# A recurrent segment loop: last K half in two banks, second scores moved, batched Q/K groups in column tiles

## The chip, the core and the metric

The kernel runs on one core of a Trainium2 chip. TensorE (PE) multiplies matrices into PSUM, which has eight banks of 512 float32 columns; VectorE (DVE) and ScalarE (ACT) read PSUM and write SBUF; GpSimd (POOL) works from SBUF to SBUF; SyncE (SP) issues the DMAs. Each engine works through its own list of instructions in order and waits on semaphores for the others. The metric is the device time of one execution in microseconds (us).

## The reference

Two layers follow one another on x of shape 1 x 2048 x 512, in bfloat16:

- Mixer A: `h = x + A(layernorm(x))`. A cuts the 2048 rows into 64 segments of 32 rows. To each segment 8 memory rows are put in front, so 40 rows. From them Q, K and V are computed for 32 heads of 128 (512 x 4096 weights each), causal softmax attention among the 40 rows (all rows see the 8 memory rows), and the output projection Wo (4096 x 512). The first 8 of the 40 output rows are the memory rows of the next segment, the other 32 are the result. So segment s + 1 can't start before the first output rows of segment s are there.
- Mixer B: `h + B(layernorm(h))`, a gated MLP: a 512 x 1792 projection with GELU, a layer norm of one half, a mixing over all 2048 rows with a 2048 x 2048 matrix, a gate, and an 896 x 512 projection.

## The kernel before, in words

After a start phase, in which weights are loaded and the first Q, K and V are made, the loop `for s in range(NSEG)` (line 945) runs over the 64 segments; a last phase does mixer B. The order of the instructions is written out by hand: the Python code records each operation with its engine, and what a recorded operation reads and writes (tokens such as a PSUM bank, or half of a tile) gives the semaphore waits. Two engines that read the same PSUM bank are also ordered one after the other. Nothing is rescheduled.

The work of a segment is split by rows of x. The recurrence needs the memory rows (8) and the first 24 rows of the segment, so these 32 rows are the stationary operand `hT` of four 32-column tiles of the PE, side by side, while 512 columns of the weights stream through each. Four such matmuls (one per tile) that run side by side are called a quad below. The last 8 rows of each segment ("ext" rows) depend on no memory and are computed in batches ahead of time: for 16 segments at once, 128 ext rows `hTe` are one operand. Their Q and K are made by "batched groups", one per segment of the loop (`qkx_group`, line 891, and `qkx_mm`, line 406: 16 matmuls of 128 x 128 over the whole array), and land in `QTx`; their V by `vx_group` and `vx_atoms`. Late segments (s from 48) have mixer B work in that place (`z2_group`).

The order of one segment on the PE:

- `QK` (line 501): Q and K of head halves b = 0 and b = 1, four quads each, in four banks. With `held` a quad uses the weights that the quad before it has loaded. Line 495 is a matmul with its weight load, line 496 one without. Among them `mem_out(s - 1, 1)` brings the second half of the memory rows.
- After each bank, `QK_evac` (512): ACT copies it to `Tst` (line 519), interleaving pairs of heads, and DVE transposes 32 x 32 blocks to `QT` or `KT` (line 532). The bank of the last K is copied and transposed in two halves, both once the bank is complete. DVE puts the mask into the scores' banks (line 544).
- `S_half(s, 0)` (546), the scores of half 0; ACT does the exponential (`sm_exp`, line 568). Four quads of V for half 0 and one for half 1; `V_evac(0)` on DVE (line 615); `sm_sums(0)`, the softmax sums by a matmul with ones (line 575 and 496); `S_half(s, 1)`; three quads of V for half 1; `sm_sums(1)`.
- ACT does a logarithm (`sm_ln`, 586) and an exponential (`sm_rcp`, 590) to get the reciprocal; the order on ACT is exp 0, ln 0, exp 1, rcp 0, ln 1, rcp 1. POOL copies the next segment's ext Q (`qx_copy`, 539) and normalises half 0 in two products (lines 594 and 598: the second for the ext columns). DVE evacuates V of half 1 and normalises half 1, in the same two products.
- The batched group in bank 3 (`XB`), then `PV_half` (lines 623 and 629) for both halves, in tiles of 32 rows. ACT and DVE bring the result out (`cT_evac`, 642 and 644), and DVE copies the batched group's bank to `QTx` (line 425).
- `WoX_mm` (707), a quad of ext V in most segments (433), `Wo` (line 495 with `f_cT`: quads of 256 columns), `part_evac` (671 on ACT, 673 on DVE), and `mem_out(s, 0)` (680, 685), the memory rows of the next segment.

Of the kernel before, what the change touches and what calls it, by code (L numbers as in the profile page):

```python
# [169 lines left out]
def fast_path(nc, st, keep, A_x, A_mem0, A_Wq, A_Wk, A_Wv, A_Wo, A_seg_len, B_w_in, B_w_sp, B_b_sp, B_w_out, out):  # L170
# [33 lines left out]
    def region(off, n):  # L204
        return arena[:, off:off + n]
# [5 lines left out]
    QTx = [region(4 * WSZ + i * QX, QX).rearrange("p (m s h k) -> p m s h k", m=2, s=CK, h=H) for i in range(2)]  # L211
# [269 lines left out]
    QKB = {(0, 0): 0, (0, 1): 1, (1, 0): 6, (1, 1): 7}  # L481
    SBK = (0, 1)
# [29 lines left out]
    def QK_evac(s, b, mi, parts=1):  # L512
        bank = QKB[(b, mi)]
        tb = mi
        n = 8 // parts
        for k in range(parts):
            tok = [("T", tb, 0), ("T", tb, 1)] if parts == 1 else [("T", tb, k)]
            cs = slice(64 * n * k, 64 * n * (k + 1))
            act(lambda e, cs=cs: e.activation(out=Tst[:, tb, cs].rearrange("p (hp i r) -> p hp i r", i=32, r=2),  # L519
                                              in_=ps[:, bank, cs].rearrange("p (hp r i) -> p hp i r", r=2, i=32), func=ACT.Copy),  # L520
                reads=[PB(bank)], writes=tok)
        for k in range(parts):
            tok = [("T", tb, 0), ("T", tb, 1)] if parts == 1 else [("T", tb, k)]
            src = Tst[:, tb, 64 * n * k:64 * n * (k + 1)].bitcast(U32)
            hs = slice(n * k, n * (k + 1))
            if mi == 0:
                dst = QT[:, b, hs, :, :].rearrange("p hp q r -> p (hp q r)").bitcast(U32).rearrange("p (hp q) -> p hp q", hp=n)[:, :, 8:40]
                wr = [("QT", b)]
            else:
                dst = KT[:, b, hs, :, :].rearrange("p hp q r -> p (hp q r)").bitcast(U32)  # L530
                wr = [("KT", b, 0), ("KT", b, 1)] if parts == 1 else [("KT", b, k)]
            dve(lambda e, dst=dst, src=src: e.transpose(out=dst, in_=src), reads=tok, writes=wr)  # L532
# [13 lines left out]
    def S_half(s, b):  # L546
        bank = SBK[b]
        j = s % CK
        buf = (s // CK) % 2
        rd = [("QT", b), ("KT", b, 0), ("KT", b, 1), ("QTe", b)]  # L550
        for g in range(4):
            for c in range(4):
                hp, r = 2 * c + g // 2, g % 2
                pe(lambda e, hp=hp, r=r, c=c, g=g: e.matmul(  # L554
                    ps[32 * c:32 * c + 32, bank, g * 40:(g + 1) * 40], lhsT=KT[:, b, hp, :, r], rhs=QT[:, b, hp, :, r],
                    start=False, stop=(g == 3), skip_group_check=True, tile_position=(0, 32 * c)),
                    reads=rd, writes=[PB(bank)])
        for c in range(4):
            h0 = 16 * b + 4 * c
            pe(lambda e, c=c, h0=h0: e.matmul(  # L560
                ps[32 * c:32 * c + 32, bank, 160:224], lhsT=QTx[buf][:, 1, j, h0:h0 + 4, :].rearrange("p h k -> p (h k)"),
                rhs=QT[:, b, 2 * c:2 * c + 2, 0:16, :].rearrange("p hp q r -> p hp r q"),
                start=False, stop=True, skip_group_check=True, tile_position=(0, 32 * c)),
                reads=rd + [("QTx", buf, 1, i) for i in range(8)], writes=[PB(bank)])
# [28 lines left out]
    def sm_norm(b, on):  # L593
        on(lambda e: e.tensor_tensor(out=E_sb[:, b, 0:160], in0=R_sb[:, b, :], in1=E_sb[:, b, 0:160], op=ALU.mult),
           reads=[("R", b), ("E", b)], writes=[("E", b)])
        ev = E_sb[:, b, 160:224].rearrange("p (g q) -> p g q", q=16)
        rv = R_sb[:, b, :].rearrange("p (g q) -> p g q", q=40)[:, :, 0:16]
        on(lambda e: e.tensor_tensor(out=ev, in0=rv, in1=ev, op=ALU.mult), reads=[("R", b), ("Ex", b)], writes=[("Ex", b)])

    def V_half(s, b, dcs=range(DC), held=None):  # L600
        bank = VB[b]
        sl = slot(s)
        for dc in dcs:
            for c in range(4):
                c0 = (16 * b + 4 * c) * DH
                pe(lambda e, dc=dc, c=c, c0=c0: tile_mm(e, ps[32 * c:32 * c + 32, bank, :], hT[:, sl, dc, :], w_v[:, dc, c0:c0 + 512],
                                                        dc == 0, dc == DC - 1, c, dc == held),
                   reads=[("hTx", (s // 4) % 3), ("hTm", s, dc // 2), ("W", 2, 2 * b), ("W", 2, 2 * b + 1)], writes=[PB(bank)])

    def V_evac(b, eng):  # L610
        bank = VB[b]
        if eng == "act":
            act(lambda e: e.activation(out=V_sb[:, b, :], in_=ps[:, bank, :], func=ACT.Copy), reads=[PB(bank)], writes=[("V", b)])
        else:
            dve(lambda e: e.tensor_copy(out=V_sb[:, b, :], in_=ps[:, bank, :]), reads=[PB(bank)], writes=[("V", b)])  # L615

    def PV_half(s, b):
        xb = s % NVX
        for g in range(4):
            for c in range(4):  # L620
# [5 lines left out]
                    reads=[("V", b), ("E", b)], writes=[PB(PVB[c])])  # L626
# [270 lines left out]

    def vx_group(ck, n):
# [12 lines left out]
    for ck, i0 in ((1, 10), (2, 0), (3, 0)):  # L911
# [3 lines left out]
        for i in range(i0, 16):  # L915
            qkx_group(ck, i)
# [28 lines left out]
    for s in range(NSEG):  # L945
# [15 lines left out]
        QK(s, 0, 0, (0, 1), 0, 3)  # L961
        if s > 0:
            mem_out(s - 1, 1)
        QK(s, 0, 1, (1, 0), 1, 2, None if s else 1)
        QK(s, 0, 0, (2, 3), 0, 3)
        QK_evac(s, 0, 0)
        mask_put(0)
        QK(s, 0, 1, (3, 2), 1, 2, 3)
        QK_evac(s, 0, 1)
        mask_put(1)  # L970
        for mi in range(2):
            QK(s, 1, mi, ((2, 0, 1, 3), (3, 0, 1, 2))[mi], (2, 3)[mi], (3, 2)[mi], (2, 3)[mi])
            lastop["qk"[mi]] = em.by_eng["pe"][-1]
            QK_evac(s, 1, mi, 1 + mi)
# [6 lines left out]
        V_half(s, 0, (0,))  # L981
        if s > 0:
# [25 lines left out]
        V_evac(1, "dve")  # L1008
        sm_norm(1, dve)
        if s == 0:  # L1010
# [1097 lines left out]
```

## Time and profile before

| | |
|---|---|
| median of 3 runs | 854.24 us (854.01 to 854.5) |
| the profiled execution | 853.86 us, its span 851.7 us |
| PE busy | 837.0 us, 98% of the span |
| DVE, ACT, POOL busy | 538.8, 427.1 and 159.8 us |
| chain that ended last | PE 95% |
| granted PE clock | 1.0 in every slice |

The span is the time from the first to the last instruction. The chain that ended last is followed back from the last instruction, at each step to what released it. A matmul's row gives the time of its start and a modelled length; matmuls overlap, so the distance from one start to the next is what a stage costs, and a PE that is always busy can still hold waits between starts.

### The profile page before, as it was taken

To read this page: it belongs to the slowest core of one execution; us is meant where nothing else is said; L and a number is where in the kernel's file an instruction comes from. 1 tells how busy PE (TensorE), PEld (TensorE's weight loads), DVE (VectorE), ACT (ScalarE), POOL (GpSimd) and SP (SyncE) were. 2 spreads that over 40 slices of the span, in tenths; PEclk is the share of its full clock that TensorE was granted. 3 is DMA by queue.
4 is the path that set the end of the run, shared out by engine and by line. 5 is a ranking of instruction groups with operands and counts; after the bars stand their busy time and mean duration, and the time that the engine had idled before them with its cause. 6 is when DMAs were issued, how large, how long until landed. Compare 5 with 4: busy or idle time off the path is not lost.

```text
span 851.7 us, 43893 instructions
## 1 busy us (share of the span) xinstructions
PE 837.0 (98%) x20921; PEld 447.0 (52%) x19133; DVE 538.8 (63%) x1256; ACT 427.1 (50%) x1151; POOL 159.8 (19%) x404
## 2 busy tenths in 40 slices
PE   6999999999999999999999999999999999999997
PEld 5754445555555555556555555555554544444443
DVE  3456677676666666676766666767666676553443
ACT  2455565656555655555655555565656566500000
POOL 5111121122121112121212121211112123200000
PEclk9999999999999999999999999999999999999999
DMA  9972322223212122121323222233322369032001
GB/s 319 379 227 59 75 56 57 54 47 82 57 34 75 34 65 62 26 72 47 64 58 85 55 74 51 81 70 85 91 57 80 96 184 366 2 112 105 33 12 40
DMA packets 105614, 77.21 MB, mean 91 GB/s; under 512 B 63304, under 2 KB 90960, under 8 KB 105424
## 3 DMA queue, kind: packets, MB, share of 16 engines
q1 hardware_dynamic: 105424, 74.35, 30.3%
q8 instruction: 159, 2.61, 1.3%
q14 instruction: 31, 0.25, 0.1%
HBM read 42.38 MB, written 21.59 MB: 75 GB/s over the span
## 4 chain that ended last, share of the span: by engine, by line
PE 95%; DMA 2%; SPq 1%; issue 0%; ACT 0%; DVE 0%; POOL 0%; POOLq 0%
PE f_ps L495 46%; PE f_ps L1183 11%; PE f_ps L496 8%; PE f_ps L414 6%; PE f_ps L707 4%; PE f_ps L1300 3%; PE f_ps L623 3%; PE f_ps L1176 2%; PE f_ps L433 2%; PE f_ps L775 2%; PE f_ps L554 1%; PE f_ps L575 1%; DMA f_arena<-in_A_Wk_dram 1%; PE f_ps L629 1%; PE f_ps L439 1%; PE f_ps L680 1%
## 5 line engine op out<-in xcount | busy, mean ns | idle before, releaser
L495 PE MATMUL f_ps<-f_arena,f_hT 128*32 128x512 bf16 x5120 | 359.5, 380 | 0.3
L495 PEld LDWEIGHTS f_ps<-f_arena,f_hT 128*32 128x32 bf16 x5120 | 117.0, 95 | 153.7 <-issue 63.0
L519 ACT ACTIVATE f_Tst<-f_ps 128x512 bf16<-128x512 f32 (+1 forms) x320 | 150.0, 510 | 77.5 <-PE f_ps L495 77.4
L495 PE MATMUL f_ps<-f_arena,f_cT 128*32 128x256 bf16 x3844 | 127.9, 272 | 0.7 <-ACT f_cT L642 0.5
L495 PEld LDWEIGHTS f_ps<-f_arena,f_cT 128*32 128x32 bf16 x3844 | 94.8, 96 | 27.3 <-ACT f_cT L642 18.2
L615 DVE CAST f_V_sb<-f_ps 128x512 bf16<-128x512 f32 x128 | 88.6, 692 | 25.4 <-PE f_ps L495 25.4
L1183 PE MATMUL f_ps<-f_arena 128*128 128x512 bf16 x448 | 100.9, 379 | 0.6 <-DMA f_arena<-wT_d 0.6
L532 DVE STREAM_TRANSPOSE f_QT<-f_Tst 128x256 uint32<-128x256 uint32 x128 | 57.0, 446 | 68.6 <-ACT f_Tst L519 68.5
L496 PE MATMUL f_ps<-f_arena,f_hT 128*32 128x512 bf16 x1024 | 99.8, 379 | 0.0
L539 POOL COPY f_QT<-f_arena 128x256 bf16<-128x256 bf16 x64 | 30.8, 482 | 313.3 <-PE f_ps L560 313.2
L642 ACT ACTIVATE f_cT<-f_ps 128x320 bf16<-128x320 f32 x128 | 49.0, 435 | 49.1 <-PE f_ps L629 49.1
L644 DVE TENSOR_SCALAR f_cT<-f_ps 128x320 bf16<-128x320 f32 x128 | 56.9, 487 | 25.4 <-PE f_ps L629 25.4
L532 DVE STREAM_TRANSPOSE f_KT<-f_Tst 128x128 uint32<-128x128 uint32 (+1 forms) x192 | 64.5, 349 | 12.9 <-ACT f_Tst L519 12.9
L1183 PEld LDWEIGHTS f_ps<-f_arena 128*128 128x128 bf16 x448 | 43.7, 98 | 53.4 <-DVE f_mv L723 1.0
L673 DVE CAST f_part<-f_ps 128x256 bf16<-128x256 f32 x64 | 27.2, 425 | 67.9 <-PE f_ps L495 67.9
L414 PE MATMUL f_ps<-f_hTe,f_arena 128*128 128x128 bf16 x1024 | 66.9, 223 | 2.2 <-DMA f_arena<-in_A_Wq_dram 1.4
L414 PEld LDWEIGHTS f_ps<-f_hTe,f_arena 128*128 128x128 bf16 x1024 | 59.1, 100 | 7.5 <-ACT f_hTe L395 1.6
L586 ACT ACTIVATE f_R_sb<-f_ps 128x160 f32<-128x160 f32 x128 | 39.1, 305 | 35.9 <-PE f_ps L496 32.7
L1189 DVE TENSOR_TENSOR f_arena<-f_ps,f_arena 128x512 f32<-128x512 f32 x28 | 19.3, 690 | 52.9 <-PE f_ps L1183 52.9
L685 ACT ACTIVATE f_hT<-f_ps 128x16 bf16<-128x16 f32 x126 | 23.3, 185 | 53.4 <-PE f_ps L680 53.0
L671 ACT ACTIVATE f_part<-f_ps 128x256 bf16<-128x256 f32 x64 | 24.6, 385 | 48.4 <-PE f_ps L495 48.4
L544 DVE CAST f_ps<-f_mask 128x224 f32<-128x224 bf16 x128 | 47.1, 368 | 0.0
(118 smaller groups left out, 1094.1 us busy)
## 6 DMA issues: line engine op xcount, KB each, us to landing
wT_d<-f_wst SPq DMA_DIRECT2D x32, 256.0 KB, 2.5
f_arena<-wT_d SPq DMA_DIRECT2D x32, 256.0 KB, 4.8
f_arena<-in_A_Wq_dram SPq DMA_DIRECT2D x4, 1024.0 KB, 8.7
f_arena<-in_A_Wk_dram SPq DMA_DIRECT2D x4, 1024.0 KB, 14.3
f_arena<-in_A_Wv_dram SPq DMA_DIRECT2D x4, 1024.0 KB, 14.5
f_arena<-in_A_Wo_dram SPq DMA_DIRECT2D x8, 512.0 KB, 9.5
f_Vx<-vext_d SPq DMA_DIRECT2D x63, 64.0 KB, 2.9
vext_d<-f_Vs SPq DMA_DIRECT2D x24, 128.0 KB, 2.0
```

The lines of the kernel that those rows point to most:

```text
L414: pe(lambda e, h=h, dc=dc, hh=hh: e.matmul(ps[:, bank, hh * 128:(hh + 1) * 128], lhsT=ws[:, dc, h * DH:(h + 1) * DH], rhs=hTe[:, ck % 3, d ...
L495: return e.matmul(out, lhsT=lhsT, rhs=rhs, start=start, stop=stop, skip_group_check=True, tile_position=(0, 32 * c))
L496: return e.add_instruction(mybir.InstMatmult(name=nc.get_next_instruction_name(), ins=[e.lower_ap(rhs), e.lower_ap(lhsT)], outs=[e.lower_a ...
L519: act(lambda e, cs=cs: e.activation(out=Tst[:, tb, cs].rearrange("p (hp i r) -> p hp i r", i=32, r=2), in_=ps[:, bank, cs].rearrange("p (h ...
L532: dve(lambda e, dst=dst, src=src: e.transpose(out=dst, in_=src), reads=tok, writes=wr)
L544: dve(lambda e: e.tensor_copy(out=ps[:, bank, 0:224], in_=mask[:, :]), reads=["mask"], writes=[PB(bank)])
L586: act(lambda e: e.activation(out=R_sb[:, b, :], in_=ps[:, bank, 224:384], func=ACT.Ln, scale=LNS), reads=[PB(bank)], writes=[("R", b)])
L615: dve(lambda e: e.tensor_copy(out=V_sb[:, b, :], in_=ps[:, bank, :]), reads=[PB(bank)], writes=[("V", b)])
L642: act(lambda e: e.activation(out=dst, in_=src, func=ACT.Copy, scale=UNSC), reads=[PB(PVB[c])], writes=[("cT", c)])
L644: dve(lambda e: e.tensor_scalar(out=dst, in0=src, scalar1=UNSC, scalar2=None, op0=ALU.mult), reads=[PB(PVB[c])], writes=[("cT", c)])
L707: pe(lambda e, h=h, g=g, i=8 * qr + bg: e.matmul(ps[32 * g:32 * g + 32, WXB, :], lhsT=cTx[:, rb % 2, i, :], rhs=w_o[:, h, :], start=(i < 4 ...
L1183: pe(lambda e: e.matmul(ps[:, bank, 0:TB], lhsT=z2[:, sc, fb * 128:(fb + 1) * 128], rhs=wTb[tb % 2][:, :, sc, :], start=(n == 0), stop=(n ...
```

## The change

In the segment loop, and in how the batched Q and K are laid out:

- The K of half 1 goes to two banks, 3 and 7 (`KB`), eight heads each, as eight half quads of 256 columns (`K1`). The first bank is complete two half quads before the second, and is copied then.
- The order of the first Q and K quads of a segment is another, with more `held` quads.
- `sm_sums(0)` and `S_half(s, 1)` come one quad of V earlier: the last V quad of half 0 comes after the scores of half 1. `sm_sums(1)` comes one quad earlier as well: one V quad of half 1 stands behind it. On ACT `sm_exp(1)` now comes ahead of `sm_ln(0)`.
- `V_evac` of half 1 is cut in two: the first 256 columns on DVE, the other 256 on ACT. Both read bank 2.
- The ext product of half 0 (`sm_normx(0)`) is taken from POOL to DVE, ahead of V's first half copy.
- 36 of the 38 batched Q/K groups of the loop are `qkr_group`: the ext rows of four segments (32 columns of `hTe`) are the stationary operand in four column tiles, and 512 weight columns stream, in four quads. The result is evacuated by an ACT copy (`pair_copy`) and a DVE transpose, in place of one DVE copy. `QTx` has another layout for it (pairs of heads interleaved), and `qx_copy` moves 128 words of 4 bytes per partition in place of 256 of 2 bytes. Which heads stand in which scores tile changes with it.

```diff
+    KB = (3, 7)
+    def K1(s, k, dc, first, last, held):
+        bank = KB[k] if s or k else 2
+        for c in range(4):
+            rhs = w_k[:, dc, :].rearrange("p (h c i) -> p c h i", c=4, i=32)[:, c, 16 + 8 * k:24 + 8 * k, :]
+            pe(lambda e, c=c, rhs=rhs: tile_mm(e, ps[32 * c:32 * c + 32, bank, 0:256], hT[:, sl, dc, :], rhs, first, last, c, held),
...
+    def pair_copy(bank, tb):
+        act(lambda e: e.activation(out=Tst[:, tb, :].rearrange("p (C gi r) -> p C gi r", C=2, r=2),
+                                   in_=ps[:, bank, :].rearrange("p (C r gi) -> p C gi r", C=2, r=2), func=ACT.Copy),
...
+    def sm_normx(b):
...
+        dve(lambda e: e.tensor_tensor(out=ev, in0=rv, in1=ev, op=ALU.mult), reads=[("R", b), ("Ex", b)], writes=[("Ex", b)])
...
+    def qkr_group(ck, mi, b, r):
+        def f():
+            for dc in range(DC):
+                for c in range(4):
+                    rhs = ws[:, dc, :].rearrange("p (h c i) -> p c h i", c=4, i=32)[:, c, 16 * b:16 * b + 16, :]
+                    pe(lambda e, dc=dc, c=c, rhs=rhs: tile_mm(e, ps[32 * c:32 * c + 32, XB, :], hTe[:, ck % 3, dc, 32 * r:32 * r + 32], rhs,
+                                                              dc == 0, dc == DC - 1, c),
...
+            def ev():
+                pair_copy(XB, 0)
+                dst = QTxU[ck % 2][:, mi, 4 * r:4 * r + 4, 8 * b:8 * b + 8, :].rearrange("p s hp k -> p hp s k")
+                dve(lambda e: e.transpose(out=dst, in_=Tst[:, 0, :].bitcast(U32)), reads=[("T", 0, 0), ("T", 0, 1)],
...
-        QK(s, 0, 0, (0, 1), 0, 3)
+        QK(s, 0, 0, (0,), 0, 3)
+        QK(s, 0, 1, (0,), 0, 2, 0)
...
+        K1(s, 0, 3, True, False, True)
+        K1(s, 1, 3, True, False, True)
+        K1(s, 0, 0, False, False, False)
+        K1(s, 1, 0, False, False, True)
+        K1(s, 0, 1, False, False, False)
+        K1(s, 0, 2, False, True, False)
+        K1_copy(s, 0)
+        K1(s, 1, 2, False, False, True)
+        K1(s, 1, 1, False, True, False)
+        K1_copy(s, 1)
+        for k in range(2):
+            K1_transpose(k)
...
-        V_half(s, 0, (1, 2, 3))
-        V_evac(0, "dve")
-        sm_sums(0)
-        sm_ln(0)
-        S_half(s, 1)
+            V_half(s, 0, (1, 2))
+            sm_sums(0)
+            S_half(s, 1)
+            V_half(s, 0, (3,))
+            V_evac(0)
         sm_exp(1)
+        sm_ln(0)
         sm_rcp(0)
-        V_half(s, 1, (1, 2, 3) if s > 0 else range(DC))
-        sm_sums(1)
+            V_half(s, 1, (3, 1), 3)
+            sm_sums(1)
+            V_half(s, 1, (2,))
...
         sm_norm(0, pool)
-        V_evac(1, "dve")
+        sm_normx(0)
+        V_evac(1, (0,))
+        V_evac(1, (1,), "act")
         sm_norm(1, dve)
+        sm_normx(1)
```

More of the change, by code (lines that the diff above doesn't have):

```diff
@@ L510, in QK @@
                    reads=[("hTx", (s // 4) % 3), ("hTm", s, dc // 2), ("W", mi, 2 * b), ("W", mi, 2 * b + 1)], writes=[PB(bank)])
[L512 to L532, printed above, removed]
@@ new lines, in QK_evac @@
+    def QK_evac(s, b, mi):
+        pair_copy(QKB[(b, mi)], mi)
+        if mi == 0:
+            dst = QT[:, b, :, :, :].rearrange("p hp q r -> p (hp q r)").bitcast(U32).rearrange("p (hp q) -> p hp q", hp=8)[:, :, 8:40]
+            wr = [("QT", b)]
+        else:
+            dst = KT[:, b, :, :, :].rearrange("p hp q r -> p (hp q r)").bitcast(U32)
+            wr = [("KT", b, 0), ("KT", b, 1)]
+        dve(lambda e: e.transpose(out=dst, in_=Tst[:, mi, :].bitcast(U32)), reads=[("T", mi, 0), ("T", mi, 1)], writes=wr)
@@ L602, in V_half @@
         sl = slot(s)
+        last = 2 if b and s else DC - 1
         for dc in dcs:
@@ L914, in fast_path @@
             vx_group(2, 1)
-        for i in range(i0, 16):
-            qkx_group(ck, i)
+        if i0:
+            qkx_group(ck, 10)
+            qkx_group(ck, 11)
+        for mi, b in ((0, 0), (0, 1), (1, 0), (1, 1))[3 if i0 else 0:]:
+            for r in range(4):
+                qkr_group(ck, mi, b, r)
     for ck, n0 in ((2, 2), (3, 0)):
```

72 lines of the change are left out of this document (50 added, 22 removed).

## The prediction

> **What bounds the kernel now.** I read the page first (busy shares and the chain), then the timeline of one segment engine by engine, then one of the last segments.
>
> ```profile
> span 851.7 us, 43893 instructions
> PE 837.0 (98%) x20921; PEld 447.0 (52%) x19133; DVE 538.8 (63%) x1256; ACT 427.1 (50%) x1151; POOL 159.8 (19%) x404
> PE 95%; DMA 2%; SPq 1%; issue 0%; ACT 0%; DVE 0%; POOL 0%; POOLq 0%
> ```
>
> PE is the bound throughout: any gain must shorten the distance between starts of matmuls. Here is the PE in a segment with a batched group (line 414), from the scores of half 0 to Wo; columns are start and length in us, then line and form. Below it is the same place in a late segment.
>
> ```profile
> 412.49 0.27 PE L554 MATMUL f_ps<-f_QT,f_KT 128*32 128x40 bf16 x16
> ...
> 412.62 0.39 PE L495 MATMUL f_ps<-f_arena,f_hT 128*32 128x512 bf16 x4
> ...
> 413.70 0.24 PE L575 MATMUL f_ps<-f_E_sb,f_ones 128*32 128x160 bf16 x4
> ...
> 413.80 0.27 PE L554 MATMUL f_ps<-f_QT,f_KT 128*32 128x40 bf16 x16
> ...
> 413.93 0.81 PE L495 MATMUL f_ps<-f_arena,f_hT 128*32 128x512 bf16 x12
> 414.62 0.25 PE L575 MATMUL f_ps<-f_E_sb,f_ones 128*32 128x160 bf16 x4
> ...
> 414.83 1.07 PE L414 MATMUL f_ps<-f_hTe,f_arena 128*128 128x128 bf16 x16
> 415.83 0.27 PE L623 MATMUL f_ps<-f_E_sb,f_V_sb 32*128 32x40 bf16 x16
> ...
> 416.04 0.27 PE L623 MATMUL f_ps<-f_E_sb,f_V_sb 32*128 32x40 bf16 x16
> 416.18 0.21 PE L629 MATMUL f_ps<-f_E_sb,f_Vx 32*128 32x64 bf16 x4
> 416.32 0.61 PE L707 MATMUL f_ps<-f_arena,f_cTx 128*32 128x512 bf16 x8
> 416.76 0.39 PE L433 MATMUL f_ps<-f_arena,f_hTe 128*32 128x512 bf16 x4
> 416.97 1.05 PE L495 MATMUL f_ps<-f_arena,f_cT 128*32 128x256 bf16 x32
> 417.85 0.28 PE L496 MATMUL f_ps<-f_arena,f_cT 128*32 128x256 bf16 x4
> ```
>
> ```profile
> 628.19 0.25 PE L575 MATMUL f_ps<-f_E_sb,f_ones 128*32 128x160 bf16 x4
> ...
> 628.30 1.12 PE L775 MATMUL f_ps<-f_arena,f_hTe 128*32 128x448 bf16 x20
> 629.35 0.27 PE L623 MATMUL f_ps<-f_E_sb,f_V_sb 32*128 32x40 bf16 x16
> ...
> 629.62 0.28 PE L623 MATMUL f_ps<-f_E_sb,f_V_sb 32*128 32x40 bf16 x16
> ...
> 629.89 0.62 PE L707 MATMUL f_ps<-f_arena,f_cTx 128*32 128x512 bf16 x8
> ```
>
> From 412.62 to 413.70 five quads of 512 columns start, so a quad costs 0.216 us, weight loads hidden; a quad of 256 columns costs 0.11 (416.97 to 417.85, eight quads). Quads at these rates cannot be shortened; fewer weight loads, as the `held` quads give, are worth nothing for that reason. What can go is where the starts lie further apart than the quads need:
>
> - The sums take 0.11 when column tiles follow (628.19 to 628.30) and 0.21 when the whole-array group follows (414.62 to 414.83): 0.10 for the switch of tile shape. The five 448-column quads need 5 x 0.189 = 0.945 and take 1.05 to the row tiles of PV: 0.105 for that switch.
> - The group's 16 matmuls take 1.00 (414.83 to 415.83), where four quads would take 0.86.
> - PV of half 0 takes 0.21 (415.83 to 416.04), in the late segment 0.27 (629.35 to 629.62): with PV unhindered at about 0.15 there is a wait of 0.06 and 0.12 for half 1's normalised scores. Its cause is on DVE, quoted below.
>
> **The change, part by part.**
>
> *Batched groups, 36 of them.* Before: 0.10 for the switch and 1.00 = 1.10, with the switch to PV inside. After: 4 x 0.216 + 0.105 = 0.97. Gain 0.13 each, 4.8 us if what follows doesn't wait. The evacuation moves to ACT (about 0.60, by the row of line 519) and a DVE transpose.
>
> ```profile
> L519 ACT ACTIVATE f_Tst<-f_ps 128x512 bf16<-128x512 f32 x192 | 107.8, 596 | 60.7 <-PE f_ps L495 60.7
> 418.07 0.39 ACT L671 ACTIVATE f_part<-f_ps 128x256 bf16<-128x256 f32 x1 [0.89 <-PE f_ps L495]
> 419.01 0.42 DVE L673 CAST f_part<-f_ps 128x256 bf16<-128x256 f32 x1 [1.04 <-PE f_ps L495]
> ```
>
> I cost it at nothing: ACT is idle 0.89 ahead of the `part` copy on which the memory rows wait, DVE 1.04 even behind the copy that goes. In every fourth segment `WoX_evac` takes another 0.6 of that ACT gap; copies overlap, so both just fit; if they don't, up to 0.2 in nine segments, 2 us.
>
> *Scores and sums.* The rows of ACT, DVE and POOL in that segment:
>
> ```profile
> 412.71 0.66 ACT L519 ACTIVATE f_Tst<-f_ps 128x256 bf16<-128x256 f32 x2 [0.27 <-PE f_ps L495]
> 413.26 0.36 ACT L568 ACTIVATE f_E_sb<-f_ps 128x224 bf16<-128x224 f32 x1
> 414.01 0.31 ACT L586 ACTIVATE f_R_sb<-f_ps 128x160 f32<-128x160 f32 x1 [0.39 <-PE f_ps L496]
> 414.21 0.35 ACT L568 ACTIVATE f_E_sb<-f_ps 128x224 bf16<-128x224 f32 x1
> 414.46 0.33 ACT L590 ACTIVATE f_R_sb<-f_R_sb 128x160 f32<-128x160 f32 x1
> 414.94 0.30 ACT L586 ACTIVATE f_R_sb<-f_ps 128x160 f32<-128x160 f32 x1
> 415.27 0.34 ACT L590 ACTIVATE f_R_sb<-f_R_sb 128x160 f32<-128x160 f32 x1
> ```
>
> ```profile
> 413.13 0.58 DVE L532 STREAM_TRANSPOSE f_KT<-f_Tst 128x128 uint32<-128x128 uint32 x2 [0.20 <-ACT f_Tst L519]
> 413.93 0.69 DVE L615 CAST f_V_sb<-f_ps 128x512 bf16<-128x512 f32 x1 [0.21 <-PE f_ps L495]
> 414.80 0.69 DVE L615 CAST f_V_sb<-f_ps 128x512 bf16<-128x512 f32 x1 [0.19 <-PE f_ps L495]
> 415.64 0.34 DVE L594 TENSOR_TENSOR f_E_sb<-f_R_sb,f_E_sb 128x160 bf16<-128x160 f32 x1
> 415.91 0.21 DVE L598 TENSOR_TENSOR f_E_sb<-f_R_sb,f_E_sb 128x64 bf16<-128x64 f32 x1
> ```
>
> ```profile
> 414.93 0.49 POOL L594 TENSOR_TENSOR f_E_sb<-f_R_sb,f_E_sb 128x160 bf16<-128x160 f32 x1 [0.21 <-ACT f_R_sb L590]
> ```
>
> I move these rows to the new order, on this segment's clock. Eight half quads of K cost 8 x 0.11 = 0.87 to 0.88 for 0.864: scores 0 at 412.50. The first K half is complete about 0.10 before the old last quad's start, and a 256-column matmul is 0.11 shorter (0.28 against 0.39): its copy starts near 412.51, the second 0.28 later (cadence of the pair: 0.66 less one 0.38) at 412.79, exp 0 at 413.06, ending 413.42; released matmuls start some 0.05 after ACT ends (414.56 to 414.62), so 413.47. PE, now four quads after 412.63, asks for it at 413.49. Second scores: the last transpose ended 0.34 after the last copy (413.37 to 413.71), so now 413.51 plus 0.05; PE comes at 413.59. Sums 1: exp 1, with no ln ahead of it, starts about 0.35 after scores 1 (before 0.41), 413.94, ends 414.30; PE, after 0.13 and three quads, comes at 414.37. So nothing waits, with 0.02 to 0.03 to spare at each of the three places. Against 414.62 less the quad that now stands behind (0.216) that is 0.03 gained. Bounds: 0.03 gained, up to 0.1 lost per segment where the three margins fail.
>
> *From sums 1 to Wo.* Group at 414.37 + 0.11 + 0.216 = 414.70, PV of half 0 at 415.67. ACT: ln 0 414.19, rcp 0 414.53 to 414.86 (delayed by exp 1), ln 1 414.76, rcp 1 415.09 to 415.43. POOL's product 415.00 to 415.49, in time. DVE: first V copy done 414.86, ext product 414.89 to 415.10, half copy 415.02 to 415.45 (0.42 by line 673). ACT's half copy reads the same bank and is ordered behind it: 415.49 to 415.87 (0.39 by line 671). Product 1 on DVE 415.46 to 415.79, its ext product to 415.92. PV of half 1 can start at 415.84 and needs the second V half at 415.92 from its third group on; PV of half 0 is through at 415.82. So it waits about 0.04, and WoX starts at 416.13, before 416.32: 0.19 gained, of which 0.13 is the group. `cT_evac` on ACT begins after 416.13, behind the half copy that ended 415.87.
>
> In a late segment (16 of them, no group is replaced) PV 0 starts at 414.48 + 0.216 + 1.05 = 415.75 and nothing waits: from sums 1 to WoX 1.80 less the quad = 1.59, before 1.70 (628.19 to 629.89); with the 0.03, 0.14. In the nine segments whose group is ext V (five quads, PV later still) only the 0.03 to 0.04 remains, in the two with an old group 0.09.
>
> The sum: 36 x 0.19 + 16 x 0.14 + 9 x 0.04 + 2 x 0.09 = 6.8 + 2.2 + 0.4 + 0.2 = 9.6 us. The segment head (same quads on either side of `mem_out`), `qx_copy` (POOL starts nothing that is waited for) and the last phase cost nothing. The profiled execution took 853.86, 0.38 under the median: 853.86 - 9.6 = 844.3, as a median about 844.7.
>
> **A rule against it.** The ext product of half 0 now runs on DVE, released by the same rcp 0 as POOL's product. Two such products met once before:
>
> ```profile
> 649.56 0.34 POOL L598 TENSOR_TENSOR f_E_sb<-f_R_sb,f_E_sb 128x64 bf16<-128x64 f32 x1
> 649.65 0.33 DVE L598 TENSOR_TENSOR f_E_sb<-f_R_sb,f_E_sb 128x64 bf16<-128x64 f32 x1
> ```
>
> DVE's took 0.33, not 0.21, and ended 0.08 after POOL's: it stood until POOL was through. After the change POOL starts 0.14 after rcp 0 (414.79 to 414.93), DVE 0.03 after; in the quoted pair POOL was 0.09 ahead. I take it that DVE gets through first, by about 0.1. The Trainium skill, SBUF — State Buffer, section "SBUF: two separate sides", has the rule: a DVE instruction with two SBUF inputs and a GpSimd instruction that reads SBUF share one port pair as an exclusive lock, and whoever starts first keeps it for the whole instruction. The quoted pair agrees; by this rule, too, the earlier starter, here DVE, goes unhindered.
>
> **The rivals.**
>
> - *POOL wins* (slower). Then the ext product ends 0.08 after POOL's 415.49, at 415.57 in place of 415.10, V's half copies and PV 1 come 0.47 later, in 52 segments all of it and in 11 about 0.35: +28 us, 873. It decides as soon as POOL's operand reads begin before DVE's; for it speaks the quoted pair, against it the order of release.
> - *The scores wait* (slower). The margins of 0.02 to 0.03 at sums 0, scores 1 or sums 1 fail; from 0.15 per segment on (63 x 0.15 = 9.6) the gain is gone; at 0.25 it is 860. For it: three chains through ACT with almost no slack; against: each was moved with measured cadences.
> - *Only the groups gain.* The margins fail by 0.05 or so and V's late half eats the rest: 36 x 0.13 = 4.8, 849.5.
> - *No change.* The evacuation on ACT delays the `part` copy by 0.19 in each group segment and PV's wait takes the rest: 854.
>
> **How the numbers follow.** Forecast 844.7: 0.53, own range 842 to 847.5. Only the groups: 0.21. No change: 0.05. Scores wait: 0.12. POOL wins: 0.09. So faster by over 0.2% (1.7 us, about what a measurement here can tell) 0.74, same 0.05, slower 0.21. The range 842 to 856 takes in forecast, groups and no change, the start of the third, and leaves out POOL's case and long waits.
>
> **What would show it.** From sums 1 to WoX: about 1.76 in a group segment with four quads of line-495 form in it (before 1.70, with one V quad less), and no wait over 0.05 ahead of PV 1. Sums 0 0.87 after the first V quad. DVE's ext product of half 0 at 0.21, not 0.5 or more. Period of a group segment 9.93 (before 10.12). The prediction is wrong if PV of half 1 waits for ACT's V half or DVE's ext product is long, or if line 671's copy has no idle time ahead of it.

## The result, and the profile after

The changed kernel takes 846.87 us (median of 4 runs, 844.73 to 847.27), the kernel before in the same comparison 854.18 us (854.01 to 854.5). The ratio is 0.9903, with a 95% interval of 0.989 to 0.9915. The forecast was 844.7. The profiled execution took 847.18 us; the granted PE clock was 1.0 throughout.

The page's first lines and its chain of work that ended last, after:

```profile
span 845.5 us, 44512 instructions
PE 828.5 (98%) x21945; PEld 424.1 (50%) x18629; DVE 524.0 (62%) x1320; ACT 469.2 (55%) x1251; POOL 127.4 (15%) x340
...
PE 95%; DMA 2%; SPq 1%; issue 0%; DVE 0%; ACT 0%
```

PE is still the bound: 95% of the chain as before, although ACT has 42 us more work. The PE timeline of a segment with a batched group, after (start, length, line, form):

```profile
409.13 0.27 PE L568 MATMUL f_ps<-f_QT,f_KT 128*32 128x40 bf16 x16
...
409.26 0.39 PE L497 MATMUL f_ps<-f_arena,f_hT 128*32 128x512 bf16 x4
...
410.13 0.24 PE L589 MATMUL f_ps<-f_E_sb,f_ones 128*32 128x160 bf16 x4
...
410.22 0.27 PE L568 MATMUL f_ps<-f_QT,f_KT 128*32 128x40 bf16 x16
...
411.01 0.25 PE L589 MATMUL f_ps<-f_E_sb,f_ones 128*32 128x160 bf16 x4
...
411.34 1.04 PE L497 MATMUL f_ps<-f_arena,f_hTe 128*32 128x512 bf16 x16
412.31 0.27 PE L642 MATMUL f_ps<-f_E_sb,f_V_sb 32*128 32x40 bf16 x16
...
412.50 0.31 PE L642 MATMUL f_ps<-f_E_sb,f_V_sb 32*128 32x40 bf16 x16
...
412.78 0.62 PE L726 MATMUL f_ps<-f_arena,f_cTx 128*32 128x512 bf16 x8
...
419.08 0.27 PE L568 MATMUL f_ps<-f_QT,f_KT 128*32 128x40 bf16 x16
```

Read starts, not lengths. From the scores of half 0 to the same place one segment later it is 419.08 - 409.13 = 9.95. Before, that distance was 10.12, from 412.49 in the prediction's timeline to this row of the next segment:

```profile
422.61 0.27 PE L554 MATMUL f_ps<-f_QT,f_KT 128*32 128x40 bf16 x16
```

From sums 1 (411.01) to WoX (412.78) it is 1.77, with one V quad (0.216) more between than before, when it was 1.70. The four quads of the group take 0.97 to PV.

ACT, DVE and POOL in that segment, from the same timeline; brackets give the idle time before the row and what ended it:

```profile
411.56 0.22 DVE L614 TENSOR_TENSOR f_E_sb<-f_R_sb,f_E_sb 128x64 bf16<-128x64 f32 x1
...
411.67 0.49 POOL L608 TENSOR_TENSOR f_E_sb<-f_R_sb,f_E_sb 128x160 bf16<-128x160 f32 x1 [0.74 <-ACT f_R_sb L604]
...
411.70 0.42 DVE L634 CAST f_V_sb<-f_ps 128x256 bf16<-128x256 f32 x1
...
412.12 0.33 DVE L608 TENSOR_TENSOR f_E_sb<-f_R_sb,f_E_sb 128x160 bf16<-128x160 f32 x1
...
412.15 0.38 ACT L632 ACTIVATE f_V_sb<-f_ps 128x256 bf16<-128x256 f32 x1
...
413.53 0.60 ACT L534 ACTIVATE f_Tst<-f_ps 128x512 bf16<-128x512 f32 x1
...
414.53 0.38 ACT L690 ACTIVATE f_part<-f_ps 128x256 bf16<-128x256 f32 x1 [0.40 <-PE f_ps L497]
```

DVE's ext product (line 614) starts 0.11 ahead of POOL's product and takes 0.22: it goes unhindered. V's second half is copied by DVE to 412.12 and by ACT to 412.53; DVE's product of half 1 ends at 412.45, and PV of half 1 starts 0.05 later. The group's evacuation (line 534) leaves 0.40 idle ahead of the `part` copy.

A late segment, after, PE:

```profile
590.35 0.25 PE L589 MATMUL f_ps<-f_E_sb,f_ones 128*32 128x160 bf16 x4
...
591.73 0.27 PE L642 MATMUL f_ps<-f_E_sb,f_V_sb 32*128 32x40 bf16 x16
...
591.88 0.28 PE L642 MATMUL f_ps<-f_E_sb,f_V_sb 32*128 32x40 bf16 x16
...
592.13 0.62 PE L726 MATMUL f_ps<-f_arena,f_cTx 128*32 128x512 bf16 x8
```

Here PV 0 to PV 1 is 0.15 (0.27 before): the wait for half 1 is gone, and sums 1 to WoX is 1.78.

Taking the distance between the scores of half 0 of one segment and the next for all 63 pairs, the medians by kind of segment are:

| period, us | ext V group | batched group | late |
|---|---|---|---|
| before | 10.082 | 10.120 | 10.096 |
| after | 10.060 | 9.947 | 9.934 |

In two further profiles of the same changed kernel these come out within 0.002, so they are the sharpest measure here. Over the loop: 36 group segments gain 0.172 each, 15 late ones 0.162, nine with ext V 0.02, the two old groups 0.1. That is 6.2 + 2.4 + 0.2 + 0.2 = 9.0 us. The loop, from the first scores to the last, went from 647.02 to 639.28, 7.7. Nearly all of the missing 1.3 is PE standing still at single places: what segments exceed the median of their kind by (the two old groups are a kind of their own) is 2.7 in all before and 3.9 after. The largest one, after:

```profile
275.97 0.23 PE L380 MATMUL f_ps<-f_ident,f_xn 128*32 128x128 bf16 x2 [1.06 <-issue]
```

"issue" says that no semaphore's event in the trace ended the wait. The DMA records of the trace do tell what came just before it. The page's table of DMA queues has a queue that carries instructions (packets, MB, share of the DMA engines):

```profile
q8 instruction: 161, 2.64, 1.4%
```

That is 16 KB a packet, and PE has 40745 records in this profile (matmuls, weight loads and its sequencer's), so one packet to about 256 of them. In e5 and e8, with 39455 and 41249 records, q8 has 156 and 163 packets. In the loop of all 14 profiles, from segment 1 on, 50 waits of a matmul of over 0.15 us are put down to "issue". All 50 end 1.2 to 1.6 us after a packet of q8 has landed; that stretch behind a landing makes up 9% of the loop's time. And all 50 matmuls stand at the same place of a block of 256, the 191st to the 196th of PE's records, counted in the order of their starts. By this, PE stood until a block of its own instructions had come; no run was made to vary it. Segments more than 0.1 above the median of their kind hold such a late block (reached less than 1.75 us behind the landing) in 109 of 121 cases, with 41.4 of their 43.5 us; of the segments at their median about a third do.

Behind the loop, the mixing of mixer B waits longer for its first matrix columns. The waits of PE, after and then before (line waited for, in total, times, longest):

```profile
PE f_ps L1252 <- DMA f_arena<-wT_d: 2.2, 1, 2.2
```

```profile
PE f_ps L1183 <- DMA f_arena<-wT_d: 0.6, 1, 0.6
```

That phase took 161.63 us in place of 160.16. So this execution gained 7.7 in the loop and lost 1.5 behind it; with 0.4 that the first scores came sooner, the last matmul starts 6.6 us earlier, against 6.7 in the execution's time. Segment 63, whose own gain should be one late segment's, lies behind the last scores and so in that phase.

### The profile page after: what moved, and what is told of

Same layout as the page of the kernel before. It is cut to its first block, busy times and chain, and to the rows that moved or that the text cites. A ratio compares the mean times of both kernels' runs of the same rounds, so it can differ in the third digit from the quotient of the medians.

```text
span 845.5 us, 44512 instructions
## 1 busy us (share of the span) xinstructions
PE 828.5 (98%) x21945; PEld 424.1 (50%) x18629; DVE 524.0 (62%) x1320; ACT 469.2 (55%) x1251; POOL 127.4 (15%) x340
## 4 chain that ended last, share of the span: by engine, by line
PE 95%; DMA 2%; SPq 1%; issue 0%; DVE 0%; ACT 0%
PE f_ps L497 43%; PE f_ps L498 14%; PE f_ps L1252 11%; PE f_ps L726 4%; PE f_ps L1369 3%; PE f_ps L642 3%; PE f_ps L1245 2%; PE f_ps L434 2%; PE f_ps L794 2%; PE f_ps L415 2%; PE f_ps L568 1%; DMA f_arena<-in_A_Wk_dram 1%; PE f_ps L589 1%; PE f_ps L440 1%; PE f_ps L699 1%; DMA f_arena<-wT_d 1%
## 5 line engine op out<-in xcount | busy, mean ns | idle before, releaser
L497 PE MATMUL f_ps<-f_arena,f_hT 128*32 128x512 bf16 (+1 forms) x4616 | 353.3, 356 | 0.3
L498 PE MATMUL f_ps<-f_arena,f_hT 128*32 128x512 bf16 x2552 | 206.4, 336 | 0.0
L534 ACT ACTIVATE f_Tst<-f_ps 128x512 bf16<-128x512 f32 x228 | 129.4, 597 | 60.3 <-PE f_ps L497 60.3
L634 DVE CAST f_V_sb<-f_ps 128x512 bf16<-128x512 f32 (+1 forms) x128 | 71.0, 555 | 42.0 <-PE f_ps L497 42.0
L582 ACT ACTIVATE f_E_sb<-f_ps 128x224 bf16<-128x224 f32 x128 | 46.2, 361 | 36.4 <-PE f_ps L574 36.4
L553 POOL COPY f_QT<-f_arena 128x128 uint32<-128x128 uint32 x64 | 18.7, 292 | 300.0 <-PE f_ps L574 299.9
L604 ACT ACTIVATE f_R_sb<-f_R_sb 128x160 f32<-128x160 f32 x128 | 43.1, 337 | 4.0
L524 ACT ACTIVATE f_Tst<-f_ps 128x256 bf16<-128x256 f32 x128 | 42.1, 381 | 3.7
L683 POOL COPY f_cTx<-f_cT 128x256 bf16<-128x256 bf16 x64 | 25.4, 396 | 121.5 <-DVE f_cT L663 121.5
```

The lines of the kernel that those rows point to most:

```text
L497: return e.matmul(out, lhsT=lhsT, rhs=rhs, start=start, stop=stop, skip_group_check=True, tile_position=(0, 32 * c))
L498: return e.add_instruction(mybir.InstMatmult(name=nc.get_next_instruction_name(), ins=[e.lower_ap(rhs), e.lower_ap(lhsT)], outs=[e.lower_a ...
L524: act(lambda e: e.activation(out=Tst[:, 1, 256 * k:256 * k + 256].rearrange("p (gi r) -> p gi r", r=2), in_=ps[:, bank, 0:256].rearrange(" ...
L534: act(lambda e: e.activation(out=Tst[:, tb, :].rearrange("p (C gi r) -> p C gi r", C=2, r=2), in_=ps[:, bank, :].rearrange("p (C r gi) -> ...
L582: act(lambda e: e.activation(out=E_sb[:, b, :], in_=ps[:, bank, 0:224], func=ACT.Exp, scale=scale, bias=SHIFT), reads=[PB(bank)], writes=[ ...
L604: act(lambda e: e.activation(out=R_sb[:, b, :], in_=R_sb[:, b, :], func=ACT.Exp, scale=-1.0, bias=RBIAS), reads=[("R", b)], writes=[("R", b)])
```

## The experiments

The kernels were compared with the kernel before on the same chip, in three batches: its median was 853.98 for e1 to e4, 854.39 for e5 to e7 and after_again, 854.73 for the rest. after_again and after_third are the changed kernel once more, before_again the kernel before. Edits are shown against the changed kernel; all of these compute the whole reference.

| kernel | median, us | ratio, 95% interval | periods: ext V, group, late |
|---|---|---|---|
| e1_groups_alone | 853.5 | 0.9996 (0.9987 to 1.0006) | 10.078, 10.117, 10.093 |
| e2_old_groups | 848.93 | 0.9935 (0.9919 to 0.9951) | 10.060, 10.014, 9.933 |
| e3_v_uncut | 852.75 | 0.9985 (0.9972 to 0.9998) | 10.060, 10.114, 10.088 |
| e4_ext_on_pool | 854.35 | 1.0 (0.9989 to 1.0012) | 10.077, 10.106, 10.074 |
| e5_k_one_bank | 859.44 | 1.0061 (1.0044 to 1.0078) | 10.251, 10.139, 10.125 |
| e6_port_lost | 880.49 | 1.03 (1.0283 to 1.0317) | 10.527, 10.581, 10.553 |
| e7_ln_first | 852.83 | 0.9976 (0.9964 to 0.9988) | 10.088, 10.091, 10.067 |
| after_again | 847.94 | 0.9915 (0.9896 to 0.9934) | 10.062, 9.946, 9.936 |
| e8_v0_early_ln_first | 845.35 | 0.9903 (0.9889 to 0.9916) | 10.088, 9.909, 9.962 |
| e9_v0_early | 846.05 | 0.9901 (0.9886 to 0.9917) | 10.063, 9.947, 9.934 |
| before_again | 853.79 | 0.9993 (0.9983 to 1.0003) | 10.079, 10.116, 10.090 |
| after_third | 848.11 | 0.9927 (0.9912 to 0.9942) | 10.061, 9.946, 9.934 |

**The batched groups alone.** The new groups and their layout, with the loop's order, the one K bank, the uncut V copy and the ext product on POOL as before.

```diff
-        K1(s, 0, 3, True, False, True)
...
+        QK(s, 1, 1, (3, 0, 1, 2), 3, 2, 3)
...
-            V_half(s, 0, (1, 2))
+            V_half(s, 0, (1, 2, 3))
+            V_evac(0)
             sm_sums(0)
+            sm_ln(0)
             S_half(s, 1)
...
-        sm_normx(0)
-        V_evac(1, (0,))
-        V_evac(1, (1,), "act")
+        sm_normx(0, pool)
+        V_evac(1)
```

> The column-tile groups (with QTx's new layout, the ACT copy and the DVE transpose) alone, in the loop as it was before. Theory: PV of half 1 waited for half 1's normalised scores already, 1.42 us after the start of sums 1, and a group that ends 0.13 sooner does not move that; the gain is 0 to 0.5 us in all, 853.7 to 854.3, and PV of half 0 starts 0.13 sooner and then waits. Rival, costs add up: 36 x 0.13 = 4.8 us, 849.4.

The result is the time before, within 0.2 of the theory's range. The timeline of PE and DVE in e1:

```profile
353.23 0.25 PE L589 MATMUL f_ps<-f_E_sb,f_ones 128*32 128x160 bf16 x4
...
354.31 0.27 PE L642 MATMUL f_ps<-f_E_sb,f_V_sb 32*128 32x40 bf16 x16
...
354.66 0.27 PE L642 MATMUL f_ps<-f_E_sb,f_V_sb 32*128 32x40 bf16 x16
```

```profile
354.26 0.34 DVE L608 TENSOR_TENSOR f_E_sb<-f_R_sb,f_E_sb 128x160 bf16<-128x160 f32 x1 [0.15 <-ACT f_R_sb L604]
```

PV 0 starts 1.08 after sums 1, before 1.21: the group is 0.13 shorter, as forecast. But PV 1 starts 1.43 after sums 1, before 1.42, as soon as DVE's product of half 1 has ended (354.60). That product waits for ACT's reciprocal, which waits for sums 1. The chain from sums 1 to PV 1 was the bound, and the shorter group turned into a longer wait (0.35 between PV 0 and PV 1 in place of 0.21).

**The rest of the change, with the old groups.**

```diff
-        for mi, b in ((0, 0), (0, 1), (1, 0), (1, 1))[3 if i0 else 0:]:
-            for r in range(4):
-                qkr_group(ck, mi, b, r)
+        for i in range(i0, 16):
+            qkx_group(ck, i)
```

> The changed kernel with all 38 groups in the old form (whole array, one DVE copy). Theory: each group segment is 0.13 longer, but the waits of together 0.07 that the changed kernel has at PV vanish: 36 x 0.06 = 2.2 us slower than the changed kernel, 849.1. Rival, costs add up: 4.8 us slower, 851.7.

The time is the theory's within 0.2. The group period is 0.067 longer than in the changed kernel, 36 x 0.067 = 2.4 us, not 0.13. PE in e2:

```profile
352.85 0.25 PE L589 MATMUL f_ps<-f_E_sb,f_ones 128*32 128x160 bf16 x4
...
354.28 0.27 PE L642 MATMUL f_ps<-f_E_sb,f_V_sb 32*128 32x40 bf16 x16
...
354.43 0.28 PE L642 MATMUL f_ps<-f_E_sb,f_V_sb 32*128 32x40 bf16 x16
...
354.68 0.61 PE L726 MATMUL f_ps<-f_arena,f_cTx 128*32 128x512 bf16 x8
```

PV 0 comes 1.43 after sums 1 (1.30 after the change), so the old group costs its 0.13; but PV 0 to PV 1 then takes 0.15 and PV 1 to WoX 0.25, in place of 0.19 and 0.28. So 0.07 of the shorter group ends in a wait in the changed kernel too. The parts don't add: a group segment gains nothing by the groups alone, and 0.067 on top of the rest.

**V's second copy in one piece.**

```diff
-        V_evac(1, (0,))
-        V_evac(1, (1,), "act")
+        V_evac(1)
```

> The changed kernel with V of half 1 evacuated by one DVE copy. Theory: product 1 on DVE starts 0.17 later, PV of half 1 with it; 36 x 0.15 + 16 x 0.1 = 7 us slower than the changed kernel, 853.9. Rival: since the two half copies read one bank and go one after the other, cutting gains nothing: 847.

PE and DVE in e3:

```profile
354.04 0.27 PE L642 MATMUL f_ps<-f_E_sb,f_V_sb 32*128 32x40 bf16 x16
...
354.40 0.27 PE L642 MATMUL f_ps<-f_E_sb,f_V_sb 32*128 32x40 bf16 x16
```

```profile
354.03 0.32 DVE L608 TENSOR_TENSOR f_E_sb<-f_R_sb,f_E_sb 128x160 bf16<-128x160 f32 x1
```

DVE's product of half 1 stands behind the whole copy, ends at 354.35, and PV 1 waits for it: 0.36 behind PV 0 in place of 0.19. That 0.17 is nearly the whole of the gain per segment, so the rival (cutting gains nothing) is out. The median is 1.2 us below the kernel before all the same; in the profiled execution the stray waits of the loop come to 1.3 us in place of 2.7.

**The ext product of half 0 back on POOL.**

```diff
-        sm_normx(0)
+        sm_normx(0, pool)
```

> The changed kernel with the ext product of half 0 back on POOL, behind the first product. Theory: it ends 0.25 after PV of half 0 could use it, 0.15 to 0.2 of wait ahead of the ext matmuls of PV 0: 36 x 0.19 + 16 x 0.13 = 9 us slower than the changed kernel, 855.8. Rival: POOL is in time and PV 1 waits for V's half anyway: 847.

PE, POOL and DVE in e4:

```profile
355.84 0.27 PE L642 MATMUL f_ps<-f_E_sb,f_V_sb 32*128 32x40 bf16 x16
356.19 0.21 PE L648 MATMUL f_ps<-f_E_sb,f_Vx 32*128 32x64 bf16 x4
```

```profile
355.76 0.37 POOL L614 TENSOR_TENSOR f_E_sb<-f_R_sb,f_E_sb 128x64 bf16<-128x64 f32 x1
```

```profile
355.65 0.32 DVE L608 TENSOR_TENSOR f_E_sb<-f_R_sb,f_E_sb 128x160 bf16<-128x160 f32 x1
```

Now the last matmuls of PV 0 (line 648) wait for POOL: 0.35 after PV 0's start in place of 0.13. POOL's product ends at 356.13, behind its own first product and beside DVE's, and takes 0.37. The gain is gone: 854.35.

**The last K in one bank.**

```diff
-        K1(s, 0, 3, True, False, True)
...
-        K1_copy(s, 0)
-        K1(s, 1, 2, False, False, True)
-        K1(s, 1, 1, False, True, False)
+        QK(s, 1, 1, (3, 0, 1, 2), 3, 2, 3)
+        K1_copy(s, 0)
         K1_copy(s, 1)
```

> The changed kernel with the last K of a segment in one bank again, as four quads of 512 columns, copied in two halves once the bank is complete. Theory: exp 0 ends 0.2 later, so sums 0, now one quad earlier than in the kernel before, wait 0.18 in each of 63 segments, and all behind them comes later: 11 us slower than the changed kernel, 858. Rival: V quads and the softmax chain have slack, the two banks are worth nothing: 847 to 849.

PE in e5:

```profile
353.46 0.39 PE L497 MATMUL f_ps<-f_arena,f_hT 128*32 128x512 bf16 x4
...
354.51 0.25 PE L589 MATMUL f_ps<-f_E_sb,f_ones 128*32 128x160 bf16 x4
```

Sums 0 comes 1.05 after the first V quad in place of 0.87: with both K copies behind the whole bank, the exponential is 0.18 late. Every kind of segment is 0.19 longer than in the changed kernel, and the kernel 5 us slower than before. With the sums one quad earlier, the first K half has to be there earlier too. No run puts the sums and the V quads back alone, so what their new order is worth by itself is not shown.

**POOL made to win.** DVE's ext product of half 0 is ordered behind POOL's product by a semaphore.

```diff
-        sm_normx(0)
+        sm_normx(0, after=[em.by_eng["pool"][-1]])
```

> The changed kernel with the ext product of half 0 on DVE made to wait for POOL's product of half 0: the prediction's case in which POOL wins, a little dearer, since DVE starts only after POOL has ended. Theory: the product ends 0.65 later, V's half copies too, PV of half 1 waits for ACT's copy about 0.6: 52 x 0.6 + 9 x 0.5 = 36 us slower than the changed kernel, 883. Rival: DVE has enough idle time around it, under 5 us slower.

POOL, DVE and PE in e6:

```profile
367.26 0.49 POOL L608 TENSOR_TENSOR f_E_sb<-f_R_sb,f_E_sb 128x160 bf16<-128x160 f32 x1 [0.74 <-ACT f_R_sb L604]
...
367.79 0.23 DVE L614 TENSOR_TENSOR f_E_sb<-f_R_sb,f_E_sb 128x64 bf16<-128x64 f32 x1 [0.70 <-POOL f_E_sb L608]
...
368.63 0.41 PE L642 MATMUL f_ps<-f_E_sb,f_V_sb 32*128 32x40 bf16 x16 [0.36 <-DVE f_E_sb L608]
```

The kernel takes 880.49, 32.5 above after_again. That is somewhat dearer than the forecast's first rival, which it put 28 above: here DVE's product ends 0.27 behind the end of POOL's (368.02 and 367.75), since it starts only then; the rival had it end 0.08 behind.

**The logarithm of half 0 ahead of the second exponential.** The forecast's slack on ACT: with `sm_ln(0)` in its old place the first reciprocal and POOL's product come earlier.

```diff
             sm_sums(0)
+            sm_ln(0)
             S_half(s, 1)
+            sm_exp(1)
             V_half(s, 0, (3,))
             V_evac(0)
-        sm_exp(1)
-        sm_ln(0)
```

> The changed kernel with ACT in the order ln 0, exp 1 (as in the kernel before) in place of exp 1, ln 0. Theory: exp 1 starts 0.06 later and sums 1 wait 0.05 in 63 segments (3 us lost), while rcp 0 and with it the chain to PV of half 1 comes up to 0.07 sooner in 52 (up to 3.5 us won): 845.5 to 849. Rival: the order exp 1 first is what the second quad behind sums 1 lives on; ln 0 first costs 0.1 or more per segment, 853 or more.

The theory's time was missed. The rival's was met but for 0.2, though by a cause that neither named. POOL, DVE and PE in e7:

```profile
353.78 0.49 POOL L608 TENSOR_TENSOR f_E_sb<-f_R_sb,f_E_sb 128x160 bf16<-128x160 f32 x1 [0.40 <-ACT f_R_sb L604]
...
353.22 0.69 DVE L634 CAST f_V_sb<-f_ps 128x512 bf16<-128x512 f32 x1 [0.65 <-PE f_ps L497]
353.82 0.53 DVE L614 TENSOR_TENSOR f_E_sb<-f_R_sb,f_E_sb 128x64 bf16<-128x64 f32 x1
...
354.98 0.41 PE L642 MATMUL f_ps<-f_E_sb,f_V_sb 32*128 32x40 bf16 x16
355.23 0.19 PE L648 MATMUL f_ps<-f_E_sb,f_Vx 32*128 32x64 bf16 x4
```

POOL's product now starts while DVE is still copying V. DVE's ext product starts 0.04 after POOL's, takes 0.53 and ends 0.08 behind it. V's two half copies come later for it, and the third group of PV 1's matmuls, which needs ACT's half, waits: line 648 stands 0.25 behind PV 1's start in place of 0.15. It is the "POOL wins" rival, in a milder form than e6. As medians over the group segments, sums 1 to WoX is 0.117 longer than in the changed kernel, and sums 1 itself 0.027 later behind the first V quad; together that is the 0.144 of the period.

**V of half 0 early, with and without the early logarithm.** If e7's loss is only the order of DVE and POOL, the early logarithm should do no harm once DVE is free in time. In e8 and e9 all four V quads of half 0 come ahead of sums 0, and its copy with them; half 1 has three quads ahead of sums 1. e8 also has e7's order on ACT.

```diff
-            V_half(s, 0, (0,))
-            V_half(s, 1, (0,), 0)
-            V_half(s, 0, (1, 2))
+            V_half(s, 0)
+            V_evac(0)
             sm_sums(0)
+            sm_ln(0)
             S_half(s, 1)
+            sm_exp(1)
...
-            V_half(s, 1, (3, 1), 3)
+            V_half(s, 1, (0, 1, 2))
             sm_sums(1)
-            V_half(s, 1, (2,))
+            V_half(s, 1, (3,))
```

(e9 is the same without the two lines `sm_ln(0)` and `sm_exp(1)`.)

> The changed kernel with ACT in the order ln 0, exp 1 and, so that DVE stands free when rcp 0 is done, all four V quads of half 0 ahead of sums 0 (V of half 0 evacuated 0.5 us sooner) and the V of half 1 in three quads ahead of sums 1 and one behind. Theory: what made the run with ln first slow was that DVE, still on V's copy, came to the ext product 0.04 after POOL and stood until POOL was through; with DVE free it takes 0.21 again, PV of half 1 waits for nothing, and against the changed kernel 0.07 is won in 52 segments for 0.03 lost in 63: 1.5 us faster than it, 845.5. Rival: ln first costs by itself what that run lost, 5 us: 852.

> The changed kernel with the V quads alone in that order, and ACT as it was (exp 1, ln 0). Theory: DVE was free in time before, so nothing that is waited for comes sooner: within 1 us of the changed kernel. Rival: V's copy of half 0 counts, 1.5 us faster or more.

DVE, POOL and PE in e8:

```profile
349.97 0.23 DVE L614 TENSOR_TENSOR f_E_sb<-f_R_sb,f_E_sb 128x64 bf16<-128x64 f32 x1 [0.20 <-ACT f_R_sb L604]
...
350.08 0.49 POOL L608 TENSOR_TENSOR f_E_sb<-f_R_sb,f_E_sb 128x160 bf16<-128x160 f32 x1 [0.41 <-ACT f_R_sb L604]
...
349.76 0.25 PE L589 MATMUL f_ps<-f_E_sb,f_ones 128*32 128x160 bf16 x4
...
351.46 0.62 PE L726 MATMUL f_ps<-f_arena,f_cTx 128*32 128x512 bf16 x8
```

DVE is idle (0.20) when the reciprocal comes, starts 0.11 ahead of POOL and takes 0.23. Sums 1 to WoX is 1.70 here, 0.07 less than in the changed kernel: the wait at PV 1 is gone. Sums 1 is again 0.027 later, which is the price of the logarithm's place. So most of e7's loss, 0.117 of 0.144 in a group segment, is the order of DVE and POOL. Group segments are 0.037 shorter than after the change, late ones 0.028 and those with ext V 0.027 longer: 36 x 0.037 - 15 x 0.028 - 11 x 0.027 = 0.6 us gained. What was expected of e8 counted 0.07 in 52 segments, but late ones had no wait at PV 1 left to win. The medians differ by more (845.35, and 848.11 for after_third on the same chip), but their intervals touch, and e9, whose periods are those of the changed kernel, came out at 846.05 there. That e8's time is the forecast 845.5 is luck to that extent. e9's own time would fit its rival (2.1 below after_third), but its periods, equal within 0.003, fit its theory: the V quads' order alone moves nothing that is waited for. e8 is the best version measured, by 0.6 us as far as the periods show it.

**How far one execution strays.** The changed kernel and the kernel before once more.

> The changed kernel once more, unchanged. In its first profile the last phase held a wait of 2.5 us for a DMA of the mixing matrix, where the kernel before had 0.9, and stray stalls in the loop 1.0 us above those of before. Theory: both vary from execution to execution; the periods of the segments repeat within 0.01 us (9.95 with a column-tile group, 9.93 late), the wait comes out anywhere from 0.5 to 2.5. Rival: the change causes them; the wait is 2 us or more again.

> The changed kernel a third time, beside the others on this chip: 846 to 848; periods of 9.95 and 9.93 again; the wait in the last phase anywhere from 0.5 to 2.5 us, by the rival 2 or more a third time.

> The kernel before, once more, for the wait for the mixing matrix in its last phase and the stray stalls of its loop. Theory: both vary whatever the kernel, 0.5 to 2.5 us for the wait, 0.5 to 4.7 for the stalls. Rival: the kernel before stays under 1 us of wait.

The stall of line 380 is in each profile of the changed kernel, at 1.06, 1.05 and 0.5 us. Summed over the loop, what segments exceed their kind's median by is 3.9, 5.7 and 5.0 in the three profiles of the changed kernel, 2.7 and 2.6 in the two of the kernel before, and 0.7 to 4.2 in e1 to e9. The waits sit at a few places, and several come back at the same instruction in each profile of one kernel and elsewhere in another, as blocks of 256 instructions counted from the program's start would have it.

The wait for the mixing matrix, as the largest distance between starts where that phase begins, is 2.54, 2.30 and 0.44 for the changed kernel, 0.92 and 0.96 before, 0.50 to 1.95 in e1 to e9. So the rival of after_again (2 us or more again) was met there and missed in after_third, and the rival of before_again (under 1 us) was met. In before_again and in three of e1 to e9 the profile puts that wait down to DVE, not to the DMA.

## Why the prediction was right, and where it was off

- **What bounds the kernel.** Right. PE's distances between starts explain the loop: 9.0 us from the periods, less 1.2 of stray waits, comes to 7.8, and 7.7 was measured.
- **Batched groups, 0.97 in place of 1.10.** The duration is exact (411.34 to 412.31). The condition set beside it, "if what follows doesn't wait", decides: alone the groups gained nothing (e1), and beside the rest 0.067 of 0.13 (e2). "Only the groups gain", the rival at 849.5, counted 0.13 for each of them; no run shows more than 0.067. Their evacuation costs nothing, as said: 0.40 idle is left ahead of the `part` copy.
- **Scores and sums.** Right to 0.01. Sums 0 is 0.87 after the first V quad; sums 1 1.75 (forecast 414.37 - 412.63 = 1.74); the second scores 0.96 (forecast 0.96). The small margins held. e5 shows what they rest on: without the early K half each segment loses 0.19.
- **From sums 1 to WoX.** 1.77 for a forecast 1.76. The wait at PV 1 is 0.07 (0.04 between PV 0 and PV 1, 0.03 within PV 1) for a forecast 0.04. This is the mis-sized term: 0.19 was put down per group segment, 0.172 was gained in a usual one. In late segments 1.78 for 1.80, so 0.162 for 0.14; with ext V 0.02 for 0.04. e3 and e4 show that the cut V copy and the ext product on DVE are each needed for the whole of it, since either undone makes the group segment 0.16 to 0.17 longer.
- **DVE ahead of POOL.** Right: 0.11 ahead and 0.22 long, forecast 0.11 (414.89 and 415.00) and 0.21. The price of the other outcome was forecast at 28 us; e6, which goes somewhat beyond it, measured 33. The Trainium skill, SBUF — State Buffer, section "SBUF: two separate sides", calls the port pair an exclusive lock for whoever starts first. The traces after the change, of e7 and of e8 agree (0.22, 0.53 and 0.23 for the same DVE product, by which of the two started first), with the exception below. That holds segment by segment: the product took 0.22 to 0.23 in all 62 segments after the change in which it met POOL's, each time starting 0.047 to 0.113 ahead, and 0.46 to 0.55 in all 62 of e7, starting 0.02 to 0.11 behind. The prediction had one earlier meeting; the kernel before has 63 more, of DVE's line 594 and POOL's line 598. In 61 of them DVE starts 0.14 to 0.15 behind, takes 0.34 in place of 0.32, and ends 0.18 behind POOL's end.
- **The sum.** 9.6 was forecast, 9.0 came in the periods. It is 0.6 short: 36 x 0.018 = 0.65 by the group segments' term and 0.2 by the one for ext V, less 0.2 that the late segments gave more.
- **"The last phase cost nothing."** Not so in this execution: +1.5, by the wait for the mixing matrix. But the same kernel waited 0.44 there in a third profile, and slower kernels up to 1.95; the two profiles of the kernel before have 0.92 and 0.96. Whether the change makes that wait longer is open.
- **Stray waits**, nearly all of them waits for a block of instructions, were not in the sum at all. They cost 1.2 more after the change in this pair of profiles, and up to 3.1 more in the others. Where the blocks end is set by the program; why some of them land late, and more so after the change, stays open, and no kernel here was made to move them.

The profiled execution is 2.9 us above what the forecast put down for it (847.18, and 853.86 - 9.6 = 844.3): 0.6 by the sum, 1.3 by stray waits and 1.5 in the last phase, less 0.4 from the earlier first scores, 3.0 in all. The median is 2.2 above its forecast.

## What to carry to other kernels

Before counting a shorter stage as a gain, find the chain that releases the stage behind it: here 0.13 us less matmul was worth 0 or 0.067, by how long the softmax took to deliver. Parts that shorten the two ends of the same wait don't add; undoing any one of four cost between a quarter of the gain and more than all of it. Where two engines' instructions are released by the same event and exclude each other, look which one starts first, and what the loser's queue holds: a start 0.04 us behind POOL's is most of what made e7 about 5 us slower. And where a wait has no releaser, count instructions: here such waits came at one place in every 256.

## What the hardware showed that was not expected

- The recorded start doesn't fully tell who gets the ports. In the start phase of the kernel before, a DVE row begins ahead of POOL's and still loses. Its timelines of DVE and POOL:

```profile
25.05 0.65 DVE L371 TENSOR_SCALAR f_part<-f_part,f_mv,f_rs 128x512 bf16<-128x512 bf16 x1 [0.35 <-POOL f_rs L365]
```

```profile
25.07 0.47 POOL L539 COPY f_QT<-f_arena 128x256 bf16<-128x256 bf16 x1
```

  DVE begins 0.03 ahead, takes 0.65 where this line usually takes 0.41, and ends 0.15 behind POOL's end (25.70 and 25.54). All 14 profiles have this meeting with the same order and the same 0.15, also where POOL's copy is the shorter one of the changed kernel (0.29, and DVE then takes 0.47). A DVE product that started 0.047 ahead of POOL's won, in one segment after the change, and POOL's then took 0.53 in place of 0.49. So the order turns close to there, as far as these different instructions can be compared.
- POOL can be the one that stands: in e4 its ext product took 0.37 (0.31 in most segments of the kernel before) beside DVE's product, which had started 0.11 ahead and took its usual 0.32. The pair quoted in the prediction has POOL's at 0.34, when POOL was ahead.
- PE stops for 0.2 to 1.1 us with no semaphore to end it, once in some of its blocks of 256 records, 1.2 to 1.6 us after a 16 KB packet of the instruction queue has landed. The places come back from one execution of a program to the next.
